# Two queues for the last spectra, and the last inverse transform of two row groups ahead of the mixing, in a state-space and MLP block kernel

## The chip, the cores and the metric

The kernel runs on one core of one Trainium2 chip. The metric is the device time of one execution in microseconds (us); of several executions the median is given. The core has TensorE (PE in the profile; PEld is its weight load), VectorE (DVE), ScalarE (ACT), GpSimd (POOL) and SyncE (SP). Each of them takes its instructions in the order of the program. SP, ScalarE and GpSimd can also issue transfers (DMA); a transfer that an engine issues waits in that engine's queue of instructions. SBUF is the memory on the chip with 128 partitions; PSUM is the memory that TensorE writes, here used in banks of 2 KB per partition.

## The reference, cut to what matters

```python
# x: 2048 tokens x 512 features; mod: six vectors made of c
h = layernorm(x) * (1 + ca) + sa
# state-space convolution: a long kernel K per feature, by FFT
y = irfft(rfft(pad(h)) * rfft(pad(K)))[:2048] + h * Dskip
x = x + ga * y
h = layernorm(x) * (1 + cb) + sb
# mixing: shift four feature quarters by +1, -1, +2, -2 tokens
m  = gelu(layernorm(h) @ w1)          # 512 x 512
x1 = h + shifted(m) @ w2              # 512 x 512
# channels
x1 = x1 + gelu(layernorm(x1) @ w3) @ w4   # 512 x 1376, 1376 x 512
out = x + gb * x1
```

All of it is float32. Products that need the precision are made in three parts: each operand is split in a high and a low half, and high x high, high x low and low x high are added.

## The kernel before

The work runs in stages. First the convolution kernel K and the forward transform of the normalized input are made (until about 212 us). Then 16 steps, two feature halves jh by eight column blocks kc, form the spectra, multiply them and write the product to a scratch table ZT in HBM (`spectrum_u`, `spectrum_k`, `multiply`, `back`, lines 641 to 714). `spectrum_k` reads a table T3, a flipped copy of a constant table (line 655), which holds 8 KB of each partition. The last inverse transform reads ZT back and adds the result to X2, which holds x for 16 row blocks of 128 tokens. Mixing (`mix_mod1`, `mix_mod2`, `mix_norm`, `transposed`, `parts_of`, `mix_half`) runs over eight groups of two row blocks in the order 7, 0, 1, 2, 3 and later 4, 5, 6. Channels (`chan`) runs over the same eight groups; its products begin when the mixing of group 3 is done.

The order is written out by hand inside `tc.manual_schedule()` (lines 1099 to 1296): each engine's order of instructions is the order of these calls.

What the change touches:

- `load_inv(jh, k, i, q)` (line 716) loads block k of ZT[jh], or its half i, on queue q. The eight blocks of jh = 1 get their buffers from `block()` (line 616), a ring of six buffers of 4 KB per partition (pool ldp, line 610). The ring has before held the last inputs of the spectra, four blocks of jh = 0 and the two halves of the raw matrix w2 (w2r, line 1144). The latter are read until `W2l` is formed (line 1186, `V.tensor_sub`).
- `inv_half(jh, g, i, pl, name)` (line 725) is the inverse transform of row blocks 4g + 2i and 4g + 2i + 1: 16 matmuls of 256 columns into one PSUM bank of pool pl. It returns a function which, when called, has VectorE add the bank to X2 (line 733). For g = 0 and 3 it reads blocks 0, 3, 4 and 7; for g = 1 and 2 blocks 1, 2, 5 and 6. Its first matmul reads block 7 - g. The names `a00`, `a01`, `a10`, `a11`, `a20`, `a21`, `a30` stand for (g, i) with jh = 1; they are emitted on PE where they are assigned and added on VectorE where they are called.
- `keep(n)` (line 1166) issues n matmuls of 512 columns whose result nobody reads.
- psT, psw and psy are the PSUM pools of this stretch: psT has two banks (transposes, `keep`), psw two (`pm`), psy two (`py`). After them `psm` (line 1239) takes four banks for the channels stage.

In the order before, the loads of blocks 3, 7, 0 and 4 by halves are all issued by SP, then blocks 1, 5, 2 and 6 (lines 1171 to 1189). PE does `keep(6)`, the half (3, 1), a00, a30, a01, `keep(14)`. While VectorE normalizes group 7, PE waits; then it transposes group 7 (line 802; ScalarE makes the high part nh at line 809, VectorE the low part nl at line 810), and then come a10 and a11 on PE, the mixing of group 7 (`three`, lines 834 to 840), the transposes of group 0, a20, the mixing of group 0, the transposes of group 1, a21, the mixing of group 1 and so on.

Of the kernel before, what the change touches and what calls it, by code (L numbers as in the profile page):

```python
# [7 lines left out]
F32 = mybir.dt.float32  # L8
# [4 lines left out]
PSUM = bass.MemoryType.PSUM  # L13
# [89 lines left out]
def dram(t, off, ap):  # L103
    return bass.AP(tensor=t.tensor, offset=t.offset + off, ap=ap)


def body(ctx, tc, A):
    nc = tc.nc
    V, S, P, T, Y = nc.vector, nc.scalar, nc.gpsimd, nc.tensor, nc.sync
# [4 lines left out]
    def act(out, in_, f=AF.Copy, scale=1.0, bias=0.0):  # L114
        return S.activation(out, in_, f, bias=bias, scale=scale)  # L115
# [390 lines left out]
    side = {k: [] for k in range(40)}  # L506
    for k in range(8):
        w, i = ("w3", k) if k < 4 else ("w4", k - 4)
# [4 lines left out]
    for n in range(3, 6):  # L513
        k = 7 * n - 9
# [88 lines left out]
    a2 = ExitStack()  # L603
# [31 lines left out]
    vus, zis, zcs = {}, {}, {}  # L635
# [80 lines left out]
    def load_inv(jh, k, i=None, q=Y):  # L716
        if (jh, k) not in zis:
            zis[jh, k] = block() if jh or k in (1, 2, 5, 6) else zip_.tile([128, 4, 256], F32, name="zi")
        a, n = (0, 4) if i is None else (2 * i, 2)
        q.dma_start(zis[jh, k][:, a:a + n], dram(ZT[jh], (k * 4 + a) * 32768, [[256, 128], [32768, n], [1, 256]]))  # L720
# [4 lines left out]
    def inv_half(jh, g, i, pl, name):  # L725
        p = pl.tile([128, 2, 256], F32, name=name)
        for e in range(2):
            b = g * 4 + i * 2 + e
            for bp, (c, sg) in enumerate(((31 - b, 1), (15 - b, 1), (b, 0), (16 + b, 0))):
                T.matmul(p[bp * 32:bp * 32 + 32, e], FI[:, c, sg], zis[jh, c // 4][:, c % 4],  # L730
                         start=True, stop=True, skip_group_check=True)
        x = X2[:, g * 4 + i * 2:g * 4 + i * 2 + 2, jh * 256:jh * 256 + 256]
        return lambda: V.tensor_add(x, p, x)
# [59 lines left out]
    def first_stats(g):  # L793
        first_stat(2 * g)
        first_stat(2 * g + 1)

    def transposed(x):
        ps = [psT.tile([128, 2, 256], F32, name=f"pT{j}") for j in range(2)]
        for j in range(2):
            for i in range(2):  # L800
                for k in range(2 * j, 2 * j + 2):
                    T.transpose(ps[j][:, k % 2, i * 128:i * 128 + 128], x[:, i, k * 128:k * 128 + 128], ident)
        return ps

    def parts_of(ps):
        hi = [cm.tile([128, 2, 256], F32R, name=f"nh{j}") for j in range(2)]
        lo = [cm.tile([128, 2, 256], F32R, name=f"nl{j}") for j in range(2)]
        for j in range(2):
            act(hi[j], ps[j])
            V.tensor_sub(lo[j], ps[j], hi[j].bitcast(F32))  # L810
        return [hi[k // 2][:, k % 2] for k in range(4)], [lo[k // 2][:, k % 2] for k in range(4)]
# [3 lines left out]
    def mix_mod1(g):  # L815
        mh[g] = (cm.tile([128, 2, 512], F32, name="h2"), cm.tile([128, 2, 2], F32, name="mv"),
                 cm.tile([128, 2], F32, name="rs"), cm.tile([128, 2], F32, name="nm"))
        for i in range(2):
            mod1(mh[g][0][:, i], 2 * g + i)

    def mix_mod2(g, i):
        h, mv, r, nm = mh[g]
        mod2(h[:, i], 2 * g + i)
        stats(mv[:, i], h[:, i])
        rstd(r[:, i:i + 1], mv[:, i, 1:2])
        P.tensor_tensor(nm[:, i:i + 1], mv[:, i, 0:1], m_one[:, :1], op=OP.mult)
        P.tensor_tensor(nm[:, i:i + 1], nm[:, i:i + 1], r[:, i:i + 1], op=OP.mult)

    def mix_norm(g):
        h, mv, r, nm = mh[g]  # L830
        for i in range(2):
            act(h[:, i], h[:, i], AF.Identity, scale=r[:, i:i + 1], bias=nm[:, i:i + 1])
# [98 lines left out]
    def mix_half(t, hl, hf, between=None):  # L931
        p = mix_w(hl, hf, between)
        go = gop.tile([128, 2, 256], F32, name="go")
        act(go, p, AF.Gelu_apprx_tanh)
        mix_out(t, hf, go)
# [163 lines left out]
    with tc.manual_schedule():  # L1099
# [55 lines left out]
        tp = lambda name, bufs=1, **k: pool(name, bufs, reuse_waits="tile", **k)  # L1155
# [6 lines left out]
            act(W2h[:, i], w2r[i // 2][:, i % 2])  # L1162
        psT = ctx.enter_context(tp("psT", space=PSUM))
        psw = ctx.enter_context(tp("psw", 2, space=PSUM))
        psy = a2.enter_context(tp("psy", 2, space=PSUM, side="right"))
        def keep(n):
            d = psT.tile([128, 2, 256], F32, name="pT0").rearrange("p a b -> p (a b)")
            for _ in range(n):
                T.matmul(d, W1h[:, 0, :128], W1h[:, 0], start=True, stop=True)

        for k, i in ((3, 1), (0, 0)):
            load_inv(1, k, i, Y)
            load_inv(1, k + 4, i, Y)
        for k, i in ((3, 0), (0, 1)):
            load_inv(1, k, i)
            load_inv(1, k + 4, i)
# [16 lines left out]
        a00 = inv_half(1, 0, 0, psy, "py")  # L1193
        a30 = inv_half(1, 3, 0, psw, "pm")
        a01 = inv_half(1, 0, 1, psw, "pm")
        keep(14)
        mix_mod1(7)
        mix_mod2(7, 0)
        mix_mod2(7, 1)
        a00()  # L1200
        mix_norm(7)
        first_stats(0)
        a30()
# [2 lines left out]
        hl = parts_of(transposed(mh.pop(7)[0]))  # L1206
        mix_mod2(0, 0)
        mix_mod2(0, 1)
        a10 = inv_half(1, 1, 0, psy, "py")
        a11 = inv_half(1, 1, 1, psy, "py")  # L1210
        mix_half(7, hl, 0)
        mix_norm(0)
        first_stats(1)
# [4 lines left out]
        mix_mod2(1, 0)  # L1218
        mix_mod2(1, 1)
        a11()  # L1220
        a20 = inv_half(1, 2, 0, psy, "py")
        mix_half(0, hl, 0)
        mix_norm(1)
        first_stats(2)
# [1 line left out]
        mix_mod1(2)  # L1226
        mix_mod2(2, 0)
        hl = parts_of(transposed(mh.pop(1)[0]))
        a21 = inv_half(1, 2, 1, psy, "py")
        a20()  # L1230
        mix_mod2(2, 1)
        a21()
# [82 lines left out]
```

## Time and profile before

| | |
|---|---|
| median of 3 executions | 679.14 us (678.92 to 680.05) |
| the profiled execution | 679.21 us |
| its span, first to last instruction | 677.4 us |
| granted TensorE clock, mean over the span | 0.992 of full |
| TensorE busy | 633.1 us (93%) |
| VectorE busy | 496.8 us (73%) |
| ScalarE busy | 331.3 us (49%) |
| GpSimd busy | 118.4 us (17%) |
| moved by DMA | 86.42 MB, mean 128 GB/s |

The profile is one execution recorded by the hardware. Its times count from the start of the span. A row of a timeline gives the start, the duration, the engine, the line of the program, the operation, what it writes and reads (`out<-in`), the shape and, after an x, how many equal instructions were merged; in brackets stands the engine's idle time before it and what ended it. A row of waits gives who waited for whom, the total, how often, and the longest. A row of the windows gives for a stretch how long each engine was busy, the granted clock, the busy share of the 16 DMA engines and the bytes per second. The chain is followed back from the last instruction through whatever released each step.

### The profile page before, as it was taken

The numbers are of one execution on the slowest core, as the hardware profiler recorded it, in microseconds if no ns is written. First come the engines' busy times: TensorE is split into PE (matmuls) and PEld (weight loads), VectorE is DVE, ScalarE is ACT, GpSimd is POOL, SyncE is SP. The second block draws the span as 40 slices with busy tenths as digits, with TensorE's granted clock in tenths as the row PEclk, the third lists the DMA queues.
The fourth block names the chain that finished last, engine by engine and source line by source line (L and its number), as shares of the span: only waits on it lengthen the run. The fifth ranks groups of instructions, "written<-read, shape, count | busy, mean of one in ns | idle before, by whom it ended". The sixth has DMA issues, their size and how long they took to land.

```text
span 677.4 us, 16876 instructions
## 1 busy us (share of the span) xinstructions
PE 633.1 (93%) x7195; PEld 507.1 (75%) x7195; DVE 496.8 (73%) x795; ACT 331.3 (49%) x505; POOL 118.4 (17%) x238
## 2 busy tenths in 40 slices
PE   1899999999999998968999999999999999999996
PEld 0456555665568877735889899898998989898895
DVE  7899999999996897997989777454674445363622
ACT  3978998898884665722446334022141213122121
POOL 4012212212207133203842002010010000000000
PEclk9999999999999999988999999999999999999999
DMA  8602274643838899966386010110100201010001
GB/s 306 287 2 75 75 229 107 202 124 80 296 64 311 289 372 354 364 209 197 110 268 237 1 60 4 49 46 16 48 31 25 70 16 48 1 62 1 1 32 31
DMA packets 50067, 86.42 MB, mean 128 GB/s; under 512 B 4676, under 2 KB 38472, under 8 KB 47400
## 3 DMA queue, kind: packets, MB, share of 16 engines
q1 hardware_dynamic: 45048, 60.97, 28.3%
q0 software_dynamic: 4624, 23.86, 9.7%
q8 instruction: 56, 0.92, 0.6%
q10 hardware_dynamic: 320, 0.52, 0.3%
q14 instruction: 19, 0.16, 0.1%
HBM read 59.12 MB, written 32.90 MB: 136 GB/s over the span
## 4 chain that ended last, share of the span: by engine, by line
PE 73%; DVE 4%; DMA 4%; issue 3%; ACT 2%; POOL 1%; SPq 0%; ACTq 0%; DVEq 0%; POOLq 0%
PE xx L448 7%; PE pm L840 7%; PE pm L838 7%; PE pm L837 7%; PE pa L957 6%; PE pa L956 6%; PE pa L964 6%; PE pk L679 4%; PE kp L498 4%; DMA ld<-ZT 3%; PE ph L894 2%; PE ph L895 2%; PE pu L426 2%; PE ph L897 2%; PE pz L701 2%
## 5 line engine op out<-in xcount | busy, mean ns | idle before, releaser
L115 ACT ACTIVATE gh<-pm 128x512 fp32r<-128x512 f32 (+1 forms) x48 | 26.9, 560 | 199.2 <-PE pm L840 199.2
L838 PE MATMUL pm<-nh,w3l 128*128 128x256 f32 (+1 forms) x352 | 85.6, 279 | 0.1
L837 PE MATMUL pm<-nh,w3h 128*128 128x256 f32 (+1 forms) x352 | 85.7, 278 | 0.0
L948 DVE TENSOR_TENSOR gl<-gf,gh 128x512 fp32r<-128x512 f32 (+1 forms) x48 | 30.8, 642 | 68.0 <-ACT gf L115 68.0
L956 PE MATMUL pa<-w4h,gh 128*128 128x512 f32 (+1 forms) x176 | 69.5, 395 | 0.0
L957 PE MATMUL pa<-w4l,gh 128*128 128x512 f32 (+1 forms) x176 | 68.9, 392 | 0.0
L838 PEld LDWEIGHTS pm<-nh,w3l 128*128 128x128 f32 (+1 forms) x352 | 65.2, 185 | 2.1 <-DVE w3l L757 0.5
L837 PEld LDWEIGHTS pm<-nh,w3h 128*128 128x128 f32 (+1 forms) x352 | 65.3, 186 | 1.4
L764 POOL TENSOR_TENSOR rs<-mv,eps_t 128x1 f32<-128x1 f32 (+1 forms) x39 | 11.0, 281 | 274.2 <-DVE mv L770 256.2
L840 PE MATMUL pm<-nl,w3h 128*128 128x256 f32 (+1 forms) x352 | 54.8, 277 | 0.1
L964 PE MATMUL pa<-w4h,gl 128*128 128x512 f32 (+1 forms) x176 | 48.0, 390 | 0.0
L449 PE MATMUL xx<-MG,ON 64*128 64x512 f32 x160 | 47.1, 390 | 0.0
L448 PE MATMUL xx<-MG,ON 64*128 64x512 f32 x160 | 47.0, 389 | 0.0
L840 PEld LDWEIGHTS pm<-nl,w3h 128*128 128x128 f32 (+1 forms) x352 | 46.6, 185 | 0.3 <-DVE nl L810 0.3
L900 DVE TENSOR_TENSOR h<-h,ph 128x512 f32<-128x512 f32 x16 | 11.0, 687 | 45.0 <-PE ph L897 45.0
L466 DVE SCALAR_TENSOR_TENSOR e<-tr,p 128x512 f32<-128x512 f32 x64 | 41.1, 683 | 0.4 <-ACT tr L115 0.4
L498 PEld LDWEIGHTS kp<-e,e 128*32 128x32 f32 x2048 | 30.1, 110 | 12.6 <-issue 7.9
L475 DVE TENSOR_TENSOR e<-tr,p 128x1024 f32<-128x1024 f32 x32 | 39.0, 1218 | 0.0
L476 DVE TENSOR_TENSOR e<-tr,m 128x1024 f32<-128x1024 f32 x32 | 39.0, 1218 | 0.0
L115 ACT ACTIVATE p<-xx 128x1024 f32<-128x1024 f32 (+1 forms) x40 | 37.5, 980 | 2.1 <-PE xx L252 0.5
L964 PEld LDWEIGHTS pa<-w4h,gl 128*128 128x128 f32 (+1 forms) x176 | 33.0, 188 | 7.1
L115 ACT ACTIVATE tr<-xx 128x1024 f32<-128x1024 f32 x32 | 33.0, 1030 | 9.7 <-PE xx L449 7.4
(241 smaller groups left out, 1709.7 us busy)
## 6 DMA issues: line engine op xcount, KB each, us to landing
VU<-vs SPq DMA_DIRECT2D x64, 128.0 KB, 3.4
ld<-VU SPq DMA_DIRECT2D x16, 512.0 KB, 8.7
ZT<-z POOLq DMA_DIRECT2D x30, 256.0 KB, 6.3
Dw<-in_w POOLq DMA_DIRECT2D x8, 688.0 KB, 4.7
xu<-in_u SPq DMA_DIRECT2D x4, 1024.0 KB, 11.9
KX<-in_x POOLq DMA_DIRECT2D x4, 1024.0 KB, 8.6
ld<-ZT SPq DMA_DIRECT2D x8, 512.0 KB, 10.4
win<-GD SPq DMA_DIRECT2D x32, 128.0 KB, 2.5
```

Source lines behind the costliest of these rows:

```text
L115: return S.activation(out, in_, f, bias=bias, scale=scale)
L448: T.matmul(x[:, :512], la, ma, start=(i == 0), stop=(i == len(ops) - 1))
L449: T.matmul(x[:, 512:], lb, mb, start=(i == 0), stop=(i == len(ops) - 1))
L466: V.scalar_tensor_tensor(e0[:, 1, a], tr[:, 1, 0], 1.0 - 2.0 * a, mg[:, a], op0=OP.mult, op1=OP.mult)
L475: V.tensor_mul(e0[:, 0], tr[:, 0, 0:1].to_broadcast([128, 2, 512]), mg)
L498: T.matmul(kp[32 * j:32 * j + 32, (k % 2) * 4 + g], e1[:, r, d], e0[:, r, :, d * 32:d * 32 + 32], start=(r == 0), stop=(r == 1), skip_grou ...
L837: T.matmul(p, wh[:, k, c], hi[k], start=(k == 0), stop=False)
L838: T.matmul(p, wl[:, k, c], hi[k], start=False, stop=False)
L840: T.matmul(p, wh[:, k, c], lo[k], start=False, stop=(k == 3))
L956: T.matmul(acc[i], gh[:m, e, s], W4h[:m, f], start=(f == 0), stop=False)
L957: T.matmul(acc[i], gh[:m, e, s], W4l[:m, f], start=False, stop=False)
L964: T.matmul(acc[i], gl[:m, e, s], W4h[:m, f], start=False, stop=(f == 10))
```

## The change

The second load of each pair of the first four goes to ScalarE's queue (S). Blocks 1 and 5 get buffers of their own in a new pool xb of two, in the place which T3 held; so blocks 2 and 6 take the next buffers of the ring, those of the two halves of w2. psy gets four banks. a10, a11 and a20 move on PE ahead of the mixing of group 7, a21 behind the call of a00, and `keep(14)` becomes `keep(4)`. The calls which add the banks to X2 stay where they were.

```diff
-        psy = a2.enter_context(tp("psy", 2, space=PSUM, side="right"))
+        psy = a2.enter_context(tp("psy", 4, space=PSUM, side="right"))
+        xb = a2.enter_context(tp("xb", 2))
+        for k in (1, 5):
+            zis[1, k] = xb.tile([128, 4, 256], F32, name="xb")
+
...
         for k, i in ((3, 1), (0, 0)):
             load_inv(1, k, i, Y)
-            load_inv(1, k + 4, i, Y)
+            load_inv(1, k + 4, i, S)
...
         a01 = inv_half(1, 0, 1, psw, "pm")
-        keep(14)
+        a10 = inv_half(1, 1, 0, psy, "py")
+        a11 = inv_half(1, 1, 1, psy, "py")
+        a20 = inv_half(1, 2, 0, psy, "py")
+        keep(4)
         mix_mod1(7)
         mix_mod2(7, 0)
         mix_mod2(7, 1)
         a00()
+        a21 = inv_half(1, 2, 1, psy, "py")
         mix_norm(7)
...
         mix_mod2(0, 1)
-        a10 = inv_half(1, 1, 0, psy, "py")
-        a11 = inv_half(1, 1, 1, psy, "py")
         mix_half(7, hl, 0)
...
         a11()
-        a20 = inv_half(1, 2, 0, psy, "py")
         mix_half(0, hl, 0)
...
         hl = parts_of(transposed(mh.pop(1)[0]))
-        a21 = inv_half(1, 2, 1, psy, "py")
         a20()
```

## The prediction

> **What bounds the kernel now.** First the page's busy line, then the table of windows over the stretch that the change touches, then the chain, the waits and the engines' timelines there. Times are us from the span's start.
>
> ```profile
> PE 633.1 (93%) x7195; PEld 507.1 (75%) x7195; DVE 496.8 (73%) x795; ACT 331.3 (49%) x505; POOL 118.4 (17%) x238
> ```
>
> ```profile
> core 0: us, PE busy (x) PEld busy (x) DVE busy (x) ACT busy (x) POOL busy (x), PEclk, DMA share, GB/s
> 298.68:306.69 8.01, 0.00 (x1) 0.03 (x1) 6.01 (x12) 1.35 (x3) 0.00 (x0) 0.67 0.74 221
> 306.69:312.67 5.98, 5.98 (x64) 3.08 (x65) 3.51 (x8) 0.00 (x0) 1.79 (x4) 0.59 0.84 272
> 312.67:318.69 6.02, 4.72 (x26) 3.40 (x23) 5.78 (x14) 1.96 (x3) 3.99 (x12) 1.00 0.60 176
> 308.69:347.06 38.37, 35.50 (x313) 28.47 (x305) 35.97 (x74) 15.29 (x23) 24.26 (x68) 0.96 0.48 152
> 347.06:668.00 320.94, 320.74 (x2085) 291.11 (x2086) 178.99 (x297) 91.10 (x168) 26.70 (x63) 1.00 0.14 48
> ```
>
> PE is busy 93% of the span, which hides that three things set the end in turn. From 298.68 to 306.69 PE does nothing. From 308.69 to 347.06 VectorE is busy 35.97 of 38.37 us. From 347.06 on PE is busy 320.74 of 320.94 us with work that the change leaves alone. So the change is worth exactly what it moves the instant of the row at 347.06 in this chain:
>
> ```profile
> 345.83 1.18 DVE nl L810 x2
> ...
> 347.06 0.50 PE pm L840 x2
> ```
>
> There PE waits for VectorE's low part of row group 2. What sets that instant is VectorE's queue since 308.69, and what set VectorE off is a load:
>
> ```profile
> 296.50 0.61 ACTq L705
> ...
> 299.95 0.37 SPq L720
> ...
> 300.43 0.41 SPq L720
> ...
> 301.47 5.08 DMA ld<-ZT
> ```
>
> ```profile
> PE py L730 <- DMA ld<-ZT: 8.0, 1, 8.0
> ```
>
> Four loads of 256 KB are issued by SP, about 0.5 us apart; the fourth lands at 301.47 + 5.08 = 306.55, and PE's 8.0 us wait ends.
>
> **The two queues.** Two of the four loads go to ScalarE's queue. An issue there took 0.61 (L705), so the last of the four starts near 299.95 + 0.61 = 300.56 and not 301.47: 0.9 earlier. Nothing queues behind the two issues: ScalarE is busy 0.00 from 306.69 to 312.67. How much of the 0.9 reaches the landing is bounded by how full the transfer engines are:
>
> ```profile
> 301.00:302.00 1.00, 0.00 (x0) 0.00 (x0) 1.00 (x3) 0.00 (x0) 0.00 (x0) 0.67 0.89 238
> 302.00:305.00 3.00, 0.00 (x0) 0.00 (x0) 2.69 (x5) 0.00 (x0) 0.00 (x0) 0.50 0.86 236
> 306.00:311.00 5.00, 4.31 (x44) 2.32 (x48) 1.84 (x6) 0.00 (x0) 0.69 (x2) 0.50 1.07 349
> 311.00:312.00 1.00, 1.00 (x20) 0.61 (x16) 1.00 (x2) 0.00 (x0) 0.92 (x3) 0.71 0.43 133
> 312.00:313.00 1.00, 1.00 (x17) 0.47 (x10) 1.00 (x2) 0.00 (x0) 0.18 (x1) 1.00 0.00 0
> 317.00:318.00 1.00, 0.25 (x3) 0.12 (x2) 0.97 (x4) 0.81 (x1) 0.88 (x3) 1.00 0.49 170
> ```
>
> They are 0.86 busy at 302 to 305 already, but move 236 GB/s there and 349 later. Filling those 3 us would save (349 − 236) × 3 / 349 = 1.0. Bounds: 0 (engines busy anyway) and 1.3 (slice 301 filled too); I take 0.7, nearer to the issue time saved. The Trainium skill ("DMA: Bandwidth & Descriptors", "Issuing engines are not separate DMA queues") says that loads started by several engines share the same 16 transfer engines and save only the issuing. Of these engines the 0.86 agrees; by that rule the gain is at most the 0.9 of issuing, and at the lower end the sum below would be +1.4.
>
> **The spare blocks.** Row groups 1 and 2 of the last transform read the spectra of blocks 1, 5, 2 and 6. The ring holds six buffers. Before, 1 and 5 took the two that held w2, and 2 and 6 had to wait for the transform that reads 3 and 7:
>
> ```profile
> SPq L720 <- PE pm L730: 4.8, 1, 4.8
> ...
> SPq L720 <- DMA ld<-ZT: 2.5, 1, 2.5
> ...
> SPq L720 <- DVE w2l L1186: 0.5, 1, 0.5
> ```
>
> ```profile
> 302.21 2.48 DVE L1186 TENSOR_TENSOR w2l<-ld,w2h 128x512 fp32r<-128x512 f32 x4
> ```
>
> ```profile
> 313.21 0.45 SPq L720 DMA_DIRECT2D ld<-ZT  x1
> ```
>
> ```profile
> ld<-ZT SPq DMA_DIRECT2D x2, 512.0 KB, 5.3
> ```
>
> So block 6 landed at 313.21 + 5.3 = 318.5. After, 1 and 5 have the flipped table's place, long free, and 2 and 6 take w2's buffers, free at 302.21 + 2.48 = 304.7, while earlier loads still flow. A new wait on an earlier landing (as the 2.5 above) would end by 306.6, also ahead of the flow. The last landing is then set by the bytes: the ten loads before ended in slice 311, which moved 133 KB. Two loads of 512 KB are 1,049 KB; 216 fit into that slice, the other 833 take 833 / 349 = 2.4, so the flow ends at 314.4. From flow to landing: the flow of block 6 ended near 317.5 (170 of 349 in slice 317) and it landed at 318.5, 1.0 more. That is 315.4, less the 0.7 from above: **314.7**, 3.8 earlier than now.
>
> **PE's order.** This is what stands there now:
>
> ```profile
> 306.69 3.64 PE L730 MATMUL py<-ld,FI 128*32 128x256 f32 x32 [8.01 <-DMA ld<-ZT]
> 310.08 2.66 PE L730 MATMUL pm<-ld,FI 128*32 128x256 f32 x32
> 312.67 3.47 PE L1169 MATMUL pT<-w1h 128*128 128x512 f32 x14
> ...
> 317.88 0.88 PE L802 MATMUL pT<-ident,h 128*128 128x128 f32 x6 [0.75 <-ACT h L115]
> 318.69 1.93 PE L730 MATMUL py<-ld,FI 128*32 128x256 f32 x32
> 320.56 0.39 PE L837 MATMUL pm<-nh,w1h 128*128 128x256 f32 x1
> ...
> 326.36 1.07 PE L802 MATMUL pT<-ident,h 128*128 128x128 f32 x8
> 327.36 1.07 PE L730 MATMUL py<-ld,FI 128*32 128x256 f32 x16
> ...
> 335.46 1.07 PE L730 MATMUL py<-ld,FI 128*32 128x256 f32 x16
> ```
>
> Removed behind 318.69 are 32 + 16 + 16 transform matmuls: 1.87 (318.69 to 320.56) and twice 1.0, 3.9 of PE. Ten of the 14 fillers go too: 3.47 / 14 = 0.248 each, 2.5. Ahead of group 7's transposes stand instead 48 transform matmuls, 4 fillers and, once a00 is added, 16 more. VectorE's and POOL's instructions keep their order; SP loses two issues and the late wait, and its next work is a store of mixing that follows group 7. The four banks let a10, a11, a20 start without an eviction, save a20, which needs the one near 309, and a21 that of a00, done at 316.2 by the row at 315.54; the pool that takes these banks later opens behind all evictions in the program, as before:
>
> ```profile
> 308.69 0.69 DVE L733 TENSOR_TENSOR KX<-py,KX 128x512 f32<-128x512 f32 x1 [3.99 <-PE py L730]
> ...
> 315.54 0.66 DVE L733 TENSOR_TENSOR KX<-py,KX 128x512 f32<-128x512 f32 x1
> ...
> 319.83 1.28 DVE L810 TENSOR_TENSOR nl<-pT,nh 128x512 fp32r<-128x512 f32 x2
> ...
> 327.67 1.29 DVE L810 TENSOR_TENSOR nl<-pT,nh 128x512 fp32r<-128x512 f32 x2 [0.30 <-ACT nh L115]
> ```
>
> But PE takes its instructions in order, and a10's first matmul reads block 6. The 64 matmuls ahead end at 312.67 now, near 312.2 after; PE then stands for some 2.5 until 314.7, with the transposes queued behind it. From there: 48 × 0.058 = 2.8, four fillers 1.0, a21 0.9, eight transposes 1.0: 5.7, so the transposes end at **320.4** and not 318.7.
>
> Who waits for that: ScalarE's copies, then VectorE's nl.
>
> ```profile
> 318.36 1.08 ACT L115 ACTIVATE nh<-pT 128x512 fp32r<-128x512 f32 x2 [0.53 <-PE pT L802]
> ```
>
> The first copy started 0.35 ahead of the transposes' end and takes about 0.55, so nl can start 0.2 behind that end, at 320.6. VectorE now comes to nl at 319.83 without waiting, and would come 0.7 earlier after. It stands 1.5, and nl starts 320.6 − 319.83 = **0.8 later** than now.
>
> From there VectorE's queue is unchanged. The only PE wait that it still has is the 0.30 at 327.67; ScalarE's copy there comes right behind a normalized half that itself follows VectorE, so I credit 0.1 of it. The 3.9 taken off PE buys no more: PE gets ahead and waits for VectorE. At 347.06 the sum is +0.8 − 0.1 = **+0.7**. The profiled execution took 679.21 (span 677.4 and 1.8 around it), 0.07 above the median of 679.14; so 679.9 for that execution and 679.8 as a median. With the two queues' gain at 0 it is +1.4, at 1.3 +0.1: 679.2 to 680.5.
>
> **Rivals.** *The clock falls (slower).* The clock was 1.00 until a third into slice 301 (0.67 mean), that is 301.34 (a third at 1.00, the rest at 0.50), 2.66 after PE's last matmul at 298.68. My standing time before a10 is 2.5, so this is close. At half clock 32 transform matmuls took 310.08 − 306.69 = 3.39, 0.106 each against 0.058. The clock came back at about 311.6 (slice 311 at 0.71), 4.9 after PE's start. A fall near 314.7 thus costs 48 × 0.048 = 2.3 on a10, a11, a20 alone and up to some 3 with the fillers; a return halfway makes it 1.5. All of it lies ahead of nl: +0.7 + 1.5 to 3.0, 681.3 to 682.8. For: the gap, and ten fillers gone that kept PE warm. Against: 2.5 is a little short of 2.66. The Trainium skill ("TensorE: Matmul & The Clock Gate", Part 1) wants an idle window of about 3.4 us, which runs freely; strictly, a 2.5 us gap would never be enough. The trace's fall, 2.66 after the last matmul, disagrees with the strict reading, so I leave the rival its chance.
>
> *All loads early (faster).* If the flow were at 349 from 301.2 on, 4,194 KB would end at 313.2 and land at 314.2; then nl is at 320.1 and nothing is won. To gain 1.4 the landing must come by 312.5, or PE's relief of 3.9 must count, which needs VectorE not to bound 308 to 347. Against: 35.97 of 38.37. The price is the first landing's best gain, 1.3, and the 0.30 at 327.67: −1.6, 677.5.
>
> *It does not do what it says.* If 2 and 6 still land at 318.5, a10 blocks the transposes until 318.5 + 5.7 = 324.2: +4.5, 683.6. Against: w2's buffers are free at 304.7.
>
> **How the numbers follow.** No change is within 0.2% (1.4 us), about what a measurement of this kernel can tell. Forecast with the clock kept: 0.52, of which 0.06 lies above 680.5. Clock falls: 0.30. Blocks late: 0.04. Faster: 0.14, of which 0.02 is too small to tell. So faster 0.12, same 0.48, slower 0.40. The range reaches from 678.6 into the rival with the fallen clock, to 682.2; left out are most of the faster case, the late blocks and the tail of the fallen clock, some 0.18. The forecast's own range is 679.2 to 680.5.
>
> **What would show it.** PE's first wait on a load a little under 8.0 and its end near 306; the last load landing near 314.7, not 318.5; a new wait of PE on the load before a10, about 2.5; nl of group 7 with a wait of about 1.5 and a start near 320.6; PE's idle time between 327 and 347 up by 2 to 3; the clock in slices 314 to 318 at 1.00 (forecast) or 0.50 (rival). Wrong if a10 follows a01 without a wait, if nl starts ahead of 319.8, or if the row at 347.06 moves by another amount than the total.

## The result, and the profile after

The changed kernel takes 684.09 us (median of 6, 681.14 to 685.00), the kernel before 679.21 (median of 6, 678.35 to 680.76). The ratio is 1.0063, with a 95% interval of 1.0048 to 1.0079: 3.3 to 5.4 us slower, about 4.3; the two medians lie 4.9 apart. The profiled execution took 684.56, with a span of 682.7. Ratios, here and below, leave out executions at a much lower granted clock, of which there was one: in experiment 11, 911.71 us at 0.654.

Now the same views as before. First the page's busy line and a table of windows, with the limits put where the stages of the changed kernel begin and end.

```profile
PE 633.9 (93%) x7185; PEld 507.2 (74%) x7185; DVE 497.5 (73%) x795; ACT 331.3 (49%) x505; POOL 117.9 (17%) x238
```

```profile
core 0: us, PE busy (x) PEld busy (x) DVE busy (x) ACT busy (x) POOL busy (x), PEclk, DMA share, GB/s
300.06:306.86 6.80, 0.00 (x0) 0.00 (x1) 6.02 (x12) 1.35 (x3) 0.00 (x0) 0.77 0.76 241
306.86:312.35 5.49, 5.49 (x64) 2.39 (x64) 3.01 (x7) 0.00 (x0) 1.78 (x4) 0.67 1.08 348
312.35:316.31 3.96, 0.00 (x1) 0.03 (x2) 3.82 (x8) 0.32 (x1) 1.78 (x7) 1.00 0.69 218
316.31:323.89 7.58, 7.58 (x76) 4.42 (x76) 3.68 (x9) 1.71 (x3) 2.21 (x7) 0.77 0.01 3
308.87:352.21 43.34, 35.63 (x302) 28.70 (x294) 36.15 (x74) 15.17 (x23) 24.33 (x68) 0.90 0.41 135
352.21:673.00 320.79, 320.57 (x2085) 290.65 (x2084) 179.06 (x297) 91.08 (x167) 26.05 (x62) 1.00 0.14 48
```

The last row is the old one: from there TensorE works without a gap, and about as long as before (320.79 against 320.94). The row ahead of it was 38.37 long and is 43.34: VectorE does the same 36 us of work in 5 us more. The wait in the first row has shrunk (6.80 for 8.01), a second wait of 3.96 is new, and so are two places at half clock. TensorE's timeline shows the order that came out:

```profile
306.86 3.64 PE L730 MATMUL py<-ld,FI 128*32 128x256 f32 x32 [6.80 <-DMA ld<-ZT]
310.36 1.99 PE L730 MATMUL pm<-ld,FI 128*32 128x256 f32 x32
316.31 0.41 PE L730 MATMUL py<-ld,FI 128*32 128x256 f32 x2 [3.96 <-DMA ld<-ZT]
...
320.62 1.25 PE L1173 MATMUL pT<-w1h 128*128 128x512 f32 x4
...
322.80 1.09 PE L802 MATMUL pT<-ident,h 128*128 128x128 f32 x8
```

TensorE is through with a01 at 312.35 and stands until block 6 lands. Then 48 matmuls, fillers and a21 stand ahead of the transposes of group 7, which end at 323.89. In VectorE's timeline, nl is the low part that needs these transposes:

```profile
308.87 0.69 DVE L733 TENSOR_TENSOR KX<-py,KX 128x512 f32<-128x512 f32 x1 [2.79 <-PE py L730]
...
324.12 1.29 DVE L810 TENSOR_TENSOR nl<-pT,nh 128x512 fp32r<-128x512 f32 x2 [4.03 <-ACT nh L115]
...
331.95 1.29 DVE L810 TENSOR_TENSOR nl<-pT,nh 128x512 fp32r<-128x512 f32 x2 [0.28 <-ACT nh L115]
...
350.90 1.29 DVE L810 TENSOR_TENSOR nl<-pT,nh 128x512 fp32r<-128x512 f32 x2 [0.78 <-ACT nh L115]
```

VectorE stands 4.03 for group 7 and 0.78 for group 2; before there was no wait at either. The row for group 2 before:

```profile
345.75 1.25 DVE L810 TENSOR_TENSOR nl<-pT,nh 128x512 fp32r<-128x512 f32 x2
```

From its first addition to nl of group 2 it is 350.90 − 308.87 = 42.03, before 345.75 − 308.69 = 37.06: 4.97 more. This length is the measure for all that follows, since it leaves out what happens ahead of the stretch, where executions differ by a us and more. The granted clock over four windows of 3.41 us:

```profile
313.94:317.35 3.41, 1.04 (x20) 0.81 (x24) 3.24 (x9) 0.98 (x2) 2.72 (x9) 1.00 0.31 98
317.35:320.76 3.41, 3.41 (x36) 1.77 (x25) 2.71 (x6) 0.65 (x1) 1.26 (x4) 0.50 0.00 0
341.24:344.66 3.42, 1.83 (x13) 1.56 (x13) 3.33 (x7) 0.00 (x0) 2.17 (x8) 1.00 0.52 152
344.66:348.07 3.41, 3.41 (x18) 3.41 (x17) 3.31 (x9) 2.00 (x3) 2.13 (x8) 0.50 0.95 326
```

After a window in which TensorE was busy for 1.04 of 3.41, the clock is halved for one window; after one with 1.83 again. The second place lies in the mixing of group 1, where TensorE waits for VectorE:

```profile
342.80 1.11 PE L840 MATMUL pm<-nl,w1h 128*128 128x256 f32 x4 [1.50 <-DVE nl L810]
```

Before, that wait was 0.84:

```profile
338.51 1.10 PE L840 MATMUL pm<-nl,w1h 128*128 128x256 f32 x4 [0.84 <-DVE nl L810]
```

With a20 and a21 gone from there TensorE arrives sooner, stands longer, and loses its clock.

The theory taken from this has three parts. **A**: the transposes of group 7 stand in TensorE's queue behind the load of block 6, and their lateness passes through nl to the end. **C**: TensorE's standing makes the clock fall, which doubles the matmuls ahead of the transposes. **C2**: relief of TensorE near 341 makes a second fall. The rivals: **O**, the order alone costs and the clock does not matter; **B**, the mere number of matmuls ahead of the transposes costs; **L**, the new loads cost.

### The profile page after: what moved, and what is told of

Its sections match the earlier page's. It is cut to its first block, busy times and chain, and to the rows that moved or that the text cites. A ratio compares the mean times of both kernels' runs of the same rounds, so it can differ in the third digit from the quotient of the medians.

```text
span 682.7 us, 16856 instructions
## 1 busy us (share of the span) xinstructions
PE 633.9 (93%) x7185; PEld 507.2 (74%) x7185; DVE 497.5 (73%) x795; ACT 331.3 (49%) x505; POOL 117.9 (17%) x238
## 4 chain that ended last, share of the span: by engine, by line
PE 75%; DMA 3%; DVE 3%; issue 3%; ACT 2%; POOL 1%; SPq 0%; ACTq 0%; DVEq 0%; POOLq 0%
PE xx L448 8%; PE pm L840 7%; PE pm L838 7%; PE pm L837 7%; PE pa L956 6%; PE pa L957 6%; PE pa L964 6%; PE pk L679 4%; PE kp L498 4%; PE pz L701 2%; PE ph L894 2%; PE ph L895 2%; PE pu L426 2%; PE ph L897 2%; DMA ld<-ZT 2%
## 5 line engine op out<-in xcount | busy, mean ns | idle before, releaser
L449 PE MATMUL xx<-MG,ON 64*128 64x512 f32 x160 | 48.0, 396 | 0.0
L448 PE MATMUL xx<-MG,ON 64*128 64x512 f32 x160 | 48.0, 396 | 0.0
```

The lines of the kernel that those rows point to most:

```text
L448: T.matmul(x[:, :512], la, ma, start=(i == 0), stop=(i == len(ops) - 1))
L449: T.matmul(x[:, 512:], lb, mb, start=(i == 0), stop=(i == len(ops) - 1))
```

## The experiments

Each ratio is against the kernel before in the same series, with its 95% interval; the median of the kernel before was 678.98 in the series of experiments 1 to 4, 679.41 in that of 5 to 8 and 679.39 in that of 9 to 11. The columns behind it are of the one profiled execution, which need not lie near the median (in experiment 6 it was the slowest of seven, 684.32): TensorE's wait for the first load, VectorE's waits at nl of group 7 and of group 2, and the length from VectorE's first addition to nl of group 2.

| kernel | median us | ratio | first wait | nl 7 waits | nl 2 waits | length |
|---|---|---|---|---|---|---|
| before | 679.21 | 1 | 8.01 | 0 | 0 | 37.06 |
| changed | 684.09 | 1.0063 (1.0048 to 1.0079) | 6.80 | 4.03 | 0.78 | 42.03 |
| 1 fillers ahead of a10 | 683.41 | 1.0053 (1.0036 to 1.0070) | 6.71 | 3.54 | 0.80 | 41.61 |
| 2 old places, new loads | 678.42 | 0.9987 (0.9974 to 0.9999) | 6.58 | 0 | 0 | 37.08 |
| 3 second queue alone | 677.73 | 0.9984 (0.9967 to 1.0001) | 6.85 | 0 | 0 | 37.09 |
| 4 new blocks alone | 679.02 | 0.9999 (0.9986 to 1.0011) | 7.65 | 0 | 0 | 37.09 |
| 5 blocks that have landed | 679.05 | 0.9998 (0.9984 to 1.0012) | 6.75 | 0 | 0.73 | 37.91 |
| 6 fillers at both places | 681.87 | 1.0042 (1.0024 to 1.0059) | 6.74 | 3.19 | 0 | 40.37 |
| 7 all behind the transposes | 680.30 | 1.0012 (0.9997 to 1.0028) | 6.84 | 0 | 0 | 38.57 |
| 8 no fillers | 683.36 | 1.0063 (1.0043 to 1.0084) | 6.77 | 4.94 | 0 | 42.13 |
| 9 second queue, warm start | 677.36 | 0.9979 (0.9964 to 0.9994) | 1.44 | 0 | 0 | 37.05 |
| 10 second queue once more | 679.16 | 0.9989 (0.9973 to 1.0004) | 7.00 | 0 | 0 | 37.06 |
| 11 landed blocks, fillers | 678.51 | 0.9991 (0.9977 to 1.0006) | 6.79 | 0 | 0 | 37.06 |

### 1. Fillers in the gap ahead of a10

```diff
         a01 = inv_half(1, 0, 1, psw, "pm")
+        keep(10)
         a10 = inv_half(1, 1, 0, psy, "py")
```

> Ten fillers (10 x 0.25 = 2.5 us) stand on TensorE between a01 and a10, where it stood 3.96 us for the load of block 6; everything else as in the changed kernel. Theory C (the clock falls while TensorE stands, and half speed is what costs most): the clock stays at 1.00 from its rise near 310.5 through the transform of groups 1 and 2, the 48 matmuls take 2.8 us and not 4.3, the transposes of group 7 end about 2 us earlier relative to the landing; total about +0.8 to +1.2 against before (680.0 to 680.4). Theory O (only the order of TensorE's queue behind the late load costs, the clock does not matter): as the changed kernel, about +4 to +5 (683.5 to 684.2).

Measured: 683.41, ratio 1.0053, nearly as slow as the changed kernel. TensorE and VectorE, rows of this kernel's timelines:

```profile
312.88 2.56 PE L1173 MATMUL pT<-w1h 128*128 128x512 f32 x10
317.16 0.41 PE L730 MATMUL py<-ld,FI 128*32 128x256 f32 x2 [1.72 <-DVE st L783]
319.89 1.20 PE L1173 MATMUL pT<-w1h 128*128 128x512 f32 x4
...
322.01 1.09 PE L802 MATMUL pT<-ident,h 128*128 128x128 f32 x8
```

```profile
323.34 1.29 DVE L810 TENSOR_TENSOR nl<-pT,nh 128x512 fp32r<-128x512 f32 x2 [3.54 <-ACT nh L115]
```

The clock held: 48 matmuls from 317.16 to 319.89, 2.7 and not 4.3. From a10's start to the transposes' end it is now 5.95 (317.16 to 323.11) where the changed kernel took 7.58 (316.31 to 323.89). Still nl waits 3.54, because block 6 landed later: a10 started 10.60 behind the first transform (306.56), in the changed kernel 9.45. The releaser named in the row ended nearly together with the load, which landed at 317.03. It isn't what a10 waits for: in the changed kernel the same statistics row ended at 317.37, after a10 had begun at 316.31. So theory C as I put it, with a remainder of +0.8 to +1.2, is wrong in size: the order behind the late load costs 3.5 by itself here. O is nearer, though the clock does matter where it falls: the fallen clock made 1.6 more of the way from a10's start to the transposes' end. The times alone don't show this, since the interval overlaps that of the changed kernel.

### 2. New loads, old places

```diff
-        a10 = inv_half(1, 1, 0, psy, "py")
-        a11 = inv_half(1, 1, 1, psy, "py")
-        a20 = inv_half(1, 2, 0, psy, "py")
-        keep(4)
+        keep(14)
...
-        a21 = inv_half(1, 2, 1, psy, "py")
...
         mix_mod2(0, 1)
+        a10 = inv_half(1, 1, 0, psy, "py")
+        a11 = inv_half(1, 1, 1, psy, "py")
```

a20 and a21 go back likewise.

> The new loads, the new blocks and the four banks stay; a10, a11, a20, a21 go back to their old places on TensorE and the 14 fillers come back. Theory C and theory O alike: no late load stands ahead of the transposes of group 7, so nothing of the +4.9 is left, and the first four loads land about 1.1 earlier, which VectorE's queue passes on whole: -0.7 to -1.2 (678.0 to 678.5). Theory L (the loads on two queues or the new buffers cost in themselves): still slower than before by over 1.

Measured: 678.42, ratio 0.9987, length 37.08. The whole loss is gone and the loads alone are a small gain, so L falls: the loss is all of TensorE's order, that is of the places and of the ten fillers.

### 3. The second queue alone

```diff
             load_inv(1, k, i, Y)
-            load_inv(1, k + 4, i, Y)
+            load_inv(1, k + 4, i, S)
```

> The kernel before with one edit: the second load of each of the first two pairs goes to ScalarE's queue. If the earlier first landing comes from the second queue: -0.7 to -1.2 (678.0 to 678.5), PE's wait on the load about 1.1 shorter than 8.0. If it comes from the loads of blocks 1 and 5 no longer standing in the ring: 679.2, the wait as before.

Measured: 677.73, ratio 0.9984 (0.9967 to 1.0001); in another series 0.9989 (experiment 10). First wait and first addition:

```profile
306.90 3.64 PE L730 MATMUL py<-ld,FI 128*32 128x256 f32 x32 [6.85 <-DMA ld<-ZT]
```

The wait is 1.16 shorter than 8.01, and the length is unchanged. Both intervals reach just over 1; the gain in time is about what the shorter wait gives, but by itself not settled.

### 4. The new blocks alone

This is experiment 2 with one queue.

```diff
-            load_inv(1, k + 4, i, S)
+            load_inv(1, k + 4, i, Y)
```

> Old places and one queue as before, but blocks 1 and 5 in their own buffers and four banks. All loads are issued early, the last lands near 315 instead of 318.5, and nobody waits for it: 679.2 if earlier landing alone buys nothing (theories C and O, VectorE bounds the stretch); up to 1 us less if a10 had waited for block 6 before.

Measured: 679.02, ratio 0.9999. The first wait is 7.65, the length 37.09. Earlier landing of blocks 1, 5, 2 and 6 buys nothing while nobody waits for them: before, a10 found its data in time, if only just, since block 6 landed at 318.56 and a10 began at 318.69.

### 5. The same work, with blocks that have landed

```diff
-                T.matmul(p[bp * 32:bp * 32 + 32, e], FI[:, c, sg], zis[jh, c // 4][:, c % 4],
+                T.matmul(p[bp * 32:bp * 32 + 32, e], FI[:, c, sg], zis[jh, {1: 0, 2: 3, 5: 4, 6: 7}.get(c // 4, c // 4) if jh else c // 4][:, c % 4],
```

> The changed kernel, but the transform of row groups 1 and 2 reads blocks 0, 3, 4, 7, which have landed, in place of 1, 2, 5, 6; all loads are still made, and the number and place of the matmuls are the same (the output of those rows is another). Theory A (the wait for the late load, with all that is queued behind it, puts group 7's transposes late): a10 follows a01 at once, the transposes wait for ScalarE alone, nl of group 7 starts where it started before or earlier, and most of the +4.9 goes: 678 to 679.5, the rest being a fall of the clock near 341 to 344, about +0.9. Theory B (the 48 matmuls and fillers ahead of the transposes cost by their sheer number): still above 681.

Measured: 679.05, ratio 0.9998. VectorE at groups 7 and 2, and two windows of the clock:

```profile
319.73 1.28 DVE L810 TENSOR_TENSOR nl<-pT,nh 128x512 fp32r<-128x512 f32 x2
...
346.48 1.29 DVE L810 TENSOR_TENSOR nl<-pT,nh 128x512 fp32r<-128x512 f32 x2 [0.73 <-ACT nh L115]
```

```profile
335.54:338.95 3.41, 1.73 (x10) 1.32 (x10) 2.78 (x6) 0.60 (x2) 3.23 (x9) 1.00 0.47 158
338.95:342.36 3.41, 3.33 (x15) 3.34 (x16) 3.31 (x9) 0.00 (x0) 1.14 (x5) 0.50 1.01 316
```

The same matmuls and fillers in the same places cost nothing at group 7 once their data is there. This settles A against B. What remains is the second fall: a length of 37.91, 0.85 over before, which eats most of the 1.2 that the second queue gains.

### 6. Fillers at both places

Experiment 1, and six fillers into a bank of psy (`keep2`, the same matmul as `keep`):

```diff
         hl = parts_of(transposed(mh.pop(1)[0]))
+        keep2(6)
```

> The changed kernel with ten fillers ahead of a10 and six more (6 x 0.23 = 1.4 us) behind the transposes of group 1, where TensorE, relieved of a21, stood 1.5 us for nl of group 1. Theory C2 (a window of the clock gate in which TensorE is busy little more than half halves the clock, and the relief makes such a window near 341 to 344): the clock stays at 1.00 there, nl of group 2 loses its wait of 0.8 on ScalarE, and the time is 0.9 below the 683.4 of the kernel with ten fillers alone: 682.5. Rival: the wait on ScalarE comes from the order of the work and stays, 683.4.

Measured: 681.87, ratio 1.0042. VectorE's rows:

```profile
325.04 1.29 DVE L810 TENSOR_TENSOR nl<-pT,nh 128x512 fp32r<-128x512 f32 x2 [3.19 <-ACT nh L115]
...
350.99 1.25 DVE L810 TENSOR_TENSOR nl<-pT,nh 128x512 fp32r<-128x512 f32 x2
```

The clock stays up near 341 and the wait of 0.80 at group 2 is gone, as C2 has it. The wait at group 7 is 0.35 shorter because a10 starts 10.24 behind the first transform and not 10.60; the fillers at group 1 have no part in that. The intervals of this ratio and of experiment 1's overlap; the trace's rows carry this, not the times.

### 7. All four behind the transposes of group 7

```diff
         mix_mod2(0, 1)
         a10 = inv_half(1, 1, 0, psy, "py")
         a11 = inv_half(1, 1, 1, psy, "py")
+        a20 = inv_half(1, 2, 0, psy, "py")
+        a21 = inv_half(1, 2, 1, psy, "py")
```

Against experiment 2; a20 and a21 leave their old places.

> New loads and blocks; 14 fillers as before; a10, a11, a20 and a21 all stand behind the transposes of group 7, ahead of its mixing. TensorE has 32 more transform matmuls (1.9 us) there and none later. If VectorE bounds the stretch with room to spare on TensorE: as with the old places, 678.4. If TensorE's queue is as tight there as VectorE's: the mixing of group 7 ends 1.9 later, the transposes of group 0 with it, and nl of group 0 about 1.2 to 1.5 later: 679.6 to 680.2.

Measured: 680.30, ratio 1.0012, length 38.57. The wait has moved to group 0:

```profile
329.01 1.29 DVE L810 TENSOR_TENSOR nl<-pT,nh 128x512 fp32r<-128x512 f32 x2 [1.90 <-ACT nh L115]
```

So 1.9 us more on TensorE there cost 1.5 (38.57 − 37.08): at this place it is nearly as tight as VectorE. The prediction's view of VectorE as the bound holds for taking work off TensorE, not for adding some.

### 8. Without the four fillers

```diff
-        keep(4)
```

> The changed kernel without its four fillers, 1.0 us less between a20 and the transposes of group 7. If the lateness of these transposes passes on whole (theory A): 1.0 below the changed kernel, 683.1. If the fillers keep the clock up: no gain or a loss, 684 or more.

Measured: 683.36, ratio 1.0063, the changed kernel's ratio again; nl of group 7 waits even longer:

```profile
324.22 1.29 DVE L810 TENSOR_TENSOR nl<-pT,nh 128x512 fp32r<-128x512 f32 x2 [4.94 <-ACT nh L115]
```

```profile
311.92:315.33 3.41, 0.66 (x12) 0.12 (x4) 3.27 (x7) 0.15 (x1) 1.65 (x5) 1.00 0.66 205
315.33:318.74 3.41, 2.16 (x24) 1.17 (x28) 3.31 (x9) 1.48 (x2) 2.35 (x7) 0.50 0.02 6
318.74:322.15 3.41, 3.41 (x40) 1.79 (x35) 0.54 (x1) 0.00 (x0) 0.00 (x0) 0.50 0.00 0
```

Here the window's edge fell so that TensorE was busy for 0.66 of 3.41, and the next one, with 2.16, was not full: two windows at half clock. From a10's start to nl it took 7.64 (316.58 to 324.22) against 7.81 in the changed kernel (316.31 to 324.12), so nearly all of the saved 1.0 was lost to the clock. That nl waits 0.9 longer all the same comes from a10, which starts 10.54 behind the first transform and not 9.45. A's 1.0 less does not show in the trace; the times can't decide, since a ratio of 1.0048 would lie inside the interval too.

This kernel also bears on C2. It has no fillers at group 1 either, and TensorE stands there as long as in the changed kernel, but the clock held:

```profile
342.93 1.10 PE L840 MATMUL pm<-nl,w1h 128*128 128x256 f32 x4 [1.50 <-DVE nl L810]
```

```profile
339.22:342.63 3.41, 1.97 (x14) 1.52 (x13) 2.63 (x5) 1.38 (x3) 3.25 (x9) 1.00 0.45 156
```

Experiment 7 stood 1.50 there too, with 1.85 of a window busy, and kept its clock. So the wait of 1.5 opens the way to a fall, and where the window's edges lie decides whether it comes: three of these five profiles have it (changed kernel, 1 and 5), two don't.

### 9 and 10. A warm start, and its base

From experiment 3:

```diff
-        keep(6)
+        keep(30)
```

> The kernel before with the second queue and 30 fillers in place of 6 ahead of the first transform half (3, 1), so that TensorE stands about 1 us and not 6.8 for the first load. If the clock gate looks at how busy TensorE was in each window of 3.41 us: the clock stays at 1.00, the 16 matmuls of (3, 1) take 1.0 and not 2.0, VectorE's queue starts 0.8 to 1.0 sooner than with the queue alone, and the sum against before is -1.9 to -2.1 (677.2). Rival: the fillers run past the landing or VectorE's start hangs on something else: as the queue alone, 678.1.

> The kernel with the second queue alone once more, as the base of the kernel with 30 fillers in the same series: -1.1 against before (678.1), ratio 0.998 to 0.999.

Measured: 677.36, ratio 0.9979 (0.9964 to 0.9994), and for the base 679.16, 0.9989 (0.9973 to 1.0004). TensorE and VectorE with the warm start:

```profile
296.90 7.12 PE L1169 MATMUL pT<-w1h 128*128 128x512 f32 x30
305.45 1.93 PE L730 MATMUL py<-ld,FI 128*32 128x256 f32 x32 [1.44 <-DMA ld<-ZT]
```

```profile
306.58 0.69 DVE L733 TENSOR_TENSOR KX<-py,KX 128x512 f32<-128x512 f32 x1 [2.01 <-PE py L730]
```

VectorE's first addition starts 1.13 behind TensorE (306.58 − 305.45); with the second queue alone it was 2.00 (308.90 − 306.90). The granted clock stayed at 1.00 through the stretch, as expected. This version is faster than both kernels, by 0.4 to 2.4 us against before, about 1.4; expected was 1.9 to 2.1. Its interval overlaps that of the second queue alone, so the 0.87 that the warm start adds is shown by the trace's rows and not by the times.

### 11. Landed blocks, with fillers at group 1

Experiment 5 with the six fillers of experiment 6.

> The kernel in which the transform of row groups 1 and 2 reads blocks that have landed (0, 3, 4, 7; the output of those rows is another), with six fillers behind the transposes of group 1. There the clock fell at 338.95 and nl of group 2 came 0.85 late. If the fall is of TensorE's own standing of 1.5 us: no fall, no wait at nl of group 2, ratio 0.9985 (678.2), 0.9 below the kernel without these fillers. Rival: the fall returns elsewhere or the fillers delay the mixing of group 1: 0.9998 as without them.

Measured: 678.51, ratio 0.9991 (0.9977 to 1.0006). The profiled length is back at 37.06 and the wait at group 2 is gone:

```profile
344.89 1.26 DVE L810 TENSOR_TENSOR nl<-pT,nh 128x512 fp32r<-128x512 f32 x2
```

TensorE stands 0.63 at group 1 instead of 1.50, and its window there is busy for 2.70 of 3.41, where no fall was seen in this stage. By the trace the second fall and its 0.85 come of TensorE's own standing, though experiments 7 and 8 show that the fall can stay away without fillers too. The times go the same way, but their intervals (0.9984 to 1.0012 without the fillers) overlap.

## Why the prediction was wrong

The forecast was 679.8, a change too small to tell, with a range up to 682.2; 684.09 came. The direction and the chain were right: the first load, VectorE's queue, nl of group 7 behind a10 behind block 6. Four steps failed.

**The clock.** "Forecast with the clock kept" got 0.52, because 2.5 us of standing is "a little short of 2.66". The standing was 3.96, and the clock fell at 317.35: a10 to the transposes' end took 7.58 where the sum had 5.7, so 1.9 more. With the clock kept it took 5.95 (experiment 1), so 1.6 of this is the clock and 0.25 is a sum that was short. This is the rival which had 0.30. The ground for passing it over was a length of standing; what the windows show instead is TensorE's share of a window of 3.41 us, and ten fillers fewer lower that share.

**The last landing.** The step was "less the 0.7 from above: 314.7". The second queue brings the first four loads forward but hardly the last. Last store issued to last load landed took 316.17 − 298.52 = 17.65 in the changed kernel's profile, but 18.71 in experiment 1 (298.32 to 317.03), against 17.55 in the sum (314.7 − 297.15) and 18.25 without the 0.7. With one queue and the new blocks (experiment 4) it took 18.78; with two queues and the new blocks (2, 5, 6, 7, 8 and 11) 18.2 to 18.7. By experiment 4 the sum's flow was 0.5 too short, and the second queue's gain at its end was 0.1 to 1.1 and mostly under 0.6, not 0.7; that the changed kernel's own profile lies 0.1 from the sum is luck. The first landing on the other hand gained 1.2 (8.01 to 6.80), not 0.7, so VectorE came 0.5 sooner to a wait that ended 0.1 to 1.2 later than the sum has it. That is most of the difference between 1.5 and the 3.5 of experiment 1, with the clock kept: a10 started 10.60 behind the first transform there, while the sum has 314.7 − (306.69 − 0.7) = 8.71. In the changed kernel's own profile it was 9.45, so there the fallen clock was the larger part. The Trainium skill ("DMA: Bandwidth & Descriptors", "Issuing engines are not separate DMA queues") says that a second issuing engine saves the issuing alone. With that the trace agrees roughly: relative to the last store, the last of the four was issued 1.0 sooner and TensorE's wait for them ended 1.2 sooner, while the last landing gained little.

**Relief that costs.** "The 3.9 taken off PE buys no more" is true, but I gave it no price. TensorE ahead of VectorE stood 1.50 near 342 where it had stood 0.84, the clock fell once more, and nl of group 2 waited 0.7 to 0.8 (changed kernel, experiments 1 and 5). With fillers in that place the standing was 0.63 to 0.65 and the wait was gone (experiments 6 and 11); it was also gone where the window's edges fell otherwise (experiments 7 and 8). No rival had this.

**The combination.** The fallen clock was priced on top of +0.7, with 682.8 as its end. The order alone is +3.5 at nl, so that the parts add up as follows, by the profiles: −1.2 for the first wait and +4.97 for the length, of which 4.03 is the wait at group 7 and 0.78 the one at group 2. That is +3.8; the measured change is +3.3 to +5.4. The two profiled spans differ by more, 5.3, because the first wait began 1.38 later (300.06 and 298.68), in work ahead of the change. In experiment 3, whose work up to there is that of the kernel before, it began at 300.05 too.

Right were: new blocks worth nothing by themselves (experiment 4); nothing lost or won behind nl of group 2, where TensorE works on without a gap; the wait of VectorE as the place where the loss arises (experiment 5 removes it by removing the wait for block 6 alone). What stays open is why the last load's landing varies by 1 us with the same loads (the load ahead of it varies by 0.5), and how often in the changed kernel the windows' edges fall as in the profiled execution.

## What to carry to other kernels

Work that is moved into an engine's idle time brings its own waits into that engine's queue: compare the landing of its last input with the time at which the next urgent instruction behind it is due, and not with the idle time. Filler matmuls can hold TensorE's clock, and replacing them by work that waits for a load can cost the clock as well as the time. If another engine bounds a stretch, relief of TensorE there is worth nothing, and may cost a window at half clock.

## What the hardware showed that was not expected

In these traces the clock changes on a fixed grid of 3.41 us within an execution: the falls at 317.35 and 344.66 in the changed kernel, for one, are 27.31 apart, eight windows. Around this change it goes with TensorE's busy share of the window just past. Rows of the kernel before:

```profile
297.93:301.34 3.41, 0.75 (x4) 0.27 (x2) 3.41 (x9) 2.10 (x4) 0.00 (x0) 1.00 0.51 123
304.76:308.17 3.41, 1.48 (x16) 0.90 (x20) 0.00 (x0) 0.00 (x0) 0.00 (x0) 0.50 1.05 349
315.00:318.41 3.41, 2.11 (x13) 1.33 (x12) 3.27 (x9) 1.68 (x3) 3.01 (x11) 1.00 0.77 252
```

Behind 0.75 the clock fell, behind 2.11 it did not; in the changed kernel it fell behind 1.04 and 1.83, in experiment 5 behind 1.73. So the border lies near half a window, and a wait of 1.5 us can be enough. It isn't sharp. In the changed kernel's own execution the clock held behind the window shown next, whose share is the same as at 341.24; it also held behind 1.81 in experiment 1 (315.56) and behind 1.73 in experiment 3 (298.32).

```profile
310.52:313.94 3.42, 1.83 (x32) 0.84 (x27) 2.98 (x6) 0.00 (x0) 1.68 (x4) 1.00 1.09 349
```

From 290 us on, no fall was seen behind more than 1.83 in any of the thirteen profiles, and a full clock held behind none below 1.73. A rise came behind 2.98 and more, not behind 1.48 here, nor behind 2.16 and 2.46 in experiment 8. Experiment 11 has the emptiest window that was followed by a rise:

```profile
305.39:308.81 3.42, 2.98 (x28) 1.38 (x32) 0.94 (x2) 0.00 (x0) 0.00 (x0) 0.50 1.08 346
```

The Trainium skill ("TensorE: Matmul & The Clock Gate", Part 1) puts the fall behind an idle window of about 3.4 us that runs freely; the length and the grid agree, the idleness does not.

That share isn't the whole measure. In an early stage of the changed kernel, two windows of the same view show a fall behind a window that was busy for nine tenths:

```profile
51.10:54.51 3.41, 3.07 (x13) 1.68 (x14) 3.26 (x6) 3.19 (x4) 0.00 (x0) 1.00 0.01 2
54.51:57.93 3.42, 3.42 (x26) 2.18 (x26) 3.42 (x5) 3.09 (x6) 1.98 (x3) 0.50 0.62 193
```

Experiments 1, 2, 6, 10 and 11 show such a fall too, each behind a window with 3.07 or 3.08 of 3.41, while in the changed kernel a window with 3.07 (75.00 to 78.41) was followed by none. No run here was made for that; its cause stays open.
